# Early attention products over 128 rows and an output stored by groups: predicting one change to a fused attention and MoE kernel

## The chip, the core and the metric

The kernel runs on one core of one Trainium2 chip. The metric is the device time of one execution, in microseconds (us). The engines are named as in the profile: PE is TensorE (matmuls; PEld is its weight load), DVE is VectorE, ACT is ScalarE, POOL is GpSimd, SP is SyncE, whose queue issues nearly all DMAs here. DMAs that one engine issues start in the order in which they stand in its queue, and an issue that must wait holds back those behind it.

## The reference, cut to what matters

```python
def _attn_ref(q, k, v, s):                     # 4 x 8 heads, 576 positions, head size 64
    scores = (1.0 / np.sqrt(D)) * np.matmul(q, k.transpose(0, 1, 3, 2))
    cum = np.cumsum(np.maximum(s, 0.0), axis=-1)
    bias = -(cum[:, :, :, None] - cum[:, :, None, :])
    scores = np.where(causal, -1000000000.0, scores + np.minimum(bias, 0.0))
    attn = softmax(scores)
    return np.matmul(attn, v)

def reference(**kwargs):
    x = attn_out.transpose(0, 2, 1, 3).reshape(2304, 512)
    x = _moe_ref(x)     # RMS norm, then (silu(x @ w_gate) * (x @ w_val)) @ w_out
    return _moe2_ref(x) # the same without the norm, with other weights
```

All inputs are float32; the widths are 512 (model) and 1536 (hidden).

## The kernel before, in words

The work has four parts, one after the other with overlap: attention, the first MoE's gate and value products, its output product, and the second MoE. Activations are held transposed: 128 features on the partitions, up to 512 positions along the free dimension. Most products are made from values split in two parts (names ending in H and L), in the type fp32r; the early attention products are plain float32, which the trace shows as two PE instructions per product.

**The early quads.** The first 128 positions of each head need only a 128x128 block of scores. `EarlyQuad` does four heads at a time, eight quads in all (4 batches, and heads 0 to 3 or 4 to 7). Per head, L907 multiplies q (64 rows, the head size) by k, and L910 adds the cumulated `s` by a product of a unit column with the tile `heights` (64 rows too: 32 heads, as H and L parts). Quad 0 of a batch has its data in partitions 0 to 63, quad 1 in 64 to 127, so that one load of 512 KB (L895, tile `eq`) serves both, and each product uses half of the rows of the array. Then DVE takes the minimum with the mask (L915), ACT the exponential (L920), PE transposes (L932), ACT or DVE copies out (L936, L937), PE multiplies by the values (L941, 128 rows, tile `ev`), and the result is copied to `x` (L951, L952). After four quads `normalise` (squares L975, sums L982, factors L1035 to L1085, the normalised parts L1089 to L1094) makes the operands of the first MoE for half of the 512 early positions. The products of the first MoE on these early positions (group E, L1105, 256 columns each for the first five of 12 weight blocks) follow, with tanh on ACT (L1112) and two products on DVE (L1114, L1117). Ahead of the quads PE runs ten products on a cleared tile (L543).

**Weights.** `load_gv` brings the first MoE's weights through `convert`: a load (L464, tile `raw`), a copy on ACT (L468), a merge on DVE (L470), the H part on ACT or POOL (L475, L476), the L part on DVE or POOL (L479). `raw_places` puts the raw block f into the buffers of weight block f + 2; the tiles `eq` and `ev` sit in buffers of later blocks (`early_q`, `early_v`), so a raw load waits until the early tile in its place has been used.

**The order of the work.** Every operation is entered with a priority and an estimated length. `Plan.run` steps through time with these lengths and fixes, for each engine, the order in which its instructions stand. On the chip each engine follows that order and waits where data are late.

**The end.** The second MoE's output is made by `strassen_out`, twice, in blocks of 512 columns, and `plain_out`. The columns stand in groups: group E holds the early positions of all batches, the others hold runs of positions (`SPANS`: group, first column, length, output group, place in it, token). `store_out` writes each block of 128 x 512 with one DMA per run (L1834), to the tokens' places in the transposed output, so that the host only transposes.

```python
w=[(f"out{gi}", (d0, at))], pri=-1.0e4)      # L1834: the run at..at+n of group gi
```

Of the kernel before, what the change touches and what calls it, by code (L numbers as in the profile page):

```python
# [23 lines left out]
P = 128  # L24
# [27 lines left out]
def f32(ap):  # L52
    return ap.bitcast(F32)
# [267 lines left out]
FIRST = 1  # L321
# [4 lines left out]
def tile_kernel(  # L326
# [175 lines left out]
    early_q = [buf("w", f"{z}{f}", [P, 4, 2, P], F32, "eq") for f in (10, 11) for z in "HL"]  # L502
    early_v = [buf("w", f"{z}{f}", [P, NH, 2, D], F32, "ev") for f in (8, 9) for z in "HL"]
# [9 lines left out]
    def setup():  # L513
# [4 lines left out]
        for i, v in enumerate(early_v):  # L518
            def pad(en, v=v):
                for z in range(2):  # L520
                    en.memset(v()[:, z::2, 1 - z], 0.0)
            op([(POOL, 520), (DVE, 620)], 0, pad, w=[(v, "pad")], pri=-1.2e6 + i)
        def units_(en):
            for r in (0, 64):
                en.tensor_tensor(
                    out=unit()[r:r + 64], in0=ident()[r:r + 64, r:r + NB * NH],
                    in1=ident()[r:r + 64, r + NB * NH:r + 2 * NB * NH], op=ALU.add)
        op(POOL, 300, units_, r=[ident], w=[unit], pri=-1.35e6)
# [13 lines left out]
        for _ in range(10):  # L542
# [14 lines left out]
        def cumulate(en):  # L557
# [6 lines left out]
            for r in (0, 64):  # L564
                en.tensor_copy(cumHL()[r:r + NB * NH], c32())
            for r in (NB * NH, 64 + NB * NH):
                en.tensor_tensor(out=cumHL()[r:r + NB * NH], in0=c32(),
                                 in1=f32(cumHL()[:NB * NH]), op=ALU.subtract)
        op(DVE, 1700, cumulate, r=[cum], w=[cum, cum2, c32, cumHL], pri=-1e6)
# [308 lines left out]
    class EarlyQuad:  # L878
# [5 lines left out]
        def __init__(self, i, x):  # L884
# [5 lines left out]
            self.ql, self.vl, self.p = early_q[self.b], early_v[self.b], early_p[i % 2]  # L890

        def load(self, pri):
            b, ql, vl = self.b, self.ql, self.vl
            if self.j == 0:
                op(SP, 4 * P * 1024, lambda en: en.dma_start(  # L895
                    out=ql(), in_=qe[b].rearrange("j d h z p -> (j d) h z p")), w=[ql], pri=pri)
# [4 lines left out]
        def scores(self, pri):  # L901
            pt = ps_ring("sps", 2)
            rows = slice(D * self.j, D * self.j + D)
            for h in range(4):
                c = slice(P * h, P * h + P)
                n = 4 * self.i + h
                op(PE, (0.422 * 4 * P, D), lambda en, h=h, c=c: en.matmul(  # L907
                    pt()[:, c], self.ql()[rows, h, 0], self.ql()[rows, h, 1],
                    start=True, stop=False), r=[self.ql], w=[pt], pri=pri)
                op(PE, (C_TR, D), lambda en, c=c, n=n: en.matmul(  # L910
# [1007 lines left out]
```

## Time and profile before

| | |
|---|---|
| median of 3 runs | 1071.48 us (1068.91 to 1071.85) |
| the profiled execution | 1073.27 us, of it 1071.5 us from the first to the last instruction |
| PE busy | 1051.1 us (98%) |
| DVE, ACT, POOL busy | 762.9, 631.1, 265.5 us |
| mean granted TensorE clock | 0.989 of 2.4 GHz |
| DMA | 211.01 MB, 197 GB/s over the span |

The page gives busy times for the whole span. A busy PE need not be PE at its best: a matmul's time doubles when the granted clock is 1.2 GHz instead of 2.4 GHz, and both count as busy. So the places to read are the granted clock by stretch, the length of one product in the chain of waits, and the waits of PE by stretch.

### The profile page before, as it was taken

How to read it: one execution, taken by the hardware profiler on the slowest of the kernel's cores; microseconds unless marked ns; L12 is line 12 of the kernel's file. 1: busy time of each engine (PE TensorE's matmuls, PEld its weight loads, DVE VectorE, ACT ScalarE, POOL GpSimd, SP SyncE). 2: the span in 40 equal slices, each digit the busy share in tenths (PEclk: the TensorE clock that was granted, in tenths of full speed). 3: DMA queues.
4: the chain of work that ended last, by engine and by line, in shares of the span. 5: the costliest groups of instructions: out<-in, count | busy, mean ns of one | idle time of the engine just before them, and what ended most of it. 6: DMA issues, size and time to landing. Idle time of an engine off the chain costs nothing.

```text
span 1071.5 us, 17574 instructions
## 1 busy us (share of the span) xinstructions
PE 1051.1 (98%) x5512; PEld 912.1 (85%) x5512; DVE 762.9 (71%) x1749; ACT 631.1 (59%) x1315; POOL 265.5 (25%) x351
## 2 busy tenths in 40 slices
PE   9989999999999999999999999999999999999998
PEld 8878888998999899899877889888888888887777
DVE  4578988777777887558878887656777667964552
ACT  3678887676677465334456766555665455664542
POOL 1166876345355230100000000221222122200000
PEclk9699999999999999999999999999999999999999
DMA  9464554334244685368887662676667767877663
GB/s 317 140 214 143 169 154 124 117 113 138 90 150 127 199 272 168 102 211 293 271 297 222 207 203 95 209 224 215 226 216 239 257 218 250 304 245 220 203 202 112
DMA packets 130204, 211.01 MB, mean 197 GB/s; under 512 B 22400, under 2 KB 56960, under 8 KB 130112
## 3 DMA queue, kind: packets, MB, share of 16 engines
q1 hardware_dynamic: 129488, 209.57, 60.4%
q8 instruction: 43, 0.70, 0.3%
q14 instruction: 49, 0.40, 0.1%
q10 hardware_dynamic: 624, 0.34, 0.1%
HBM read 145.29 MB, written 64.56 MB: 196 GB/s over the span
## 4 chain that ended last, share of the span: by engine, by line
PE 78%; DVE 7%; DMA 6%; issue 3%; ACT 3%; SPq 2%; POOL 1%; ACTq 0%; DVEq 0%; POOLq 0%
PE mo L1105 24%; PE mo L1467 9%; PE mo L1638 7%; PE sps L1638 6%; PE tp L778 4%; PE tp L1467 4%; PE sps L696 3%; PE tp L766 3%; PE sps L1467 2%; PE mo L1714 2%; DMA raw<-in_w_gv 2%; PE sps L1105 1%; PE tp L1105 1%; PE sps L907 1%; PE mo L941 1%
## 5 line engine op out<-in xcount | busy, mean ns | idle before, releaser
L1387 DVE TENSOR_TENSOR hL<-hh,hH 128x512 fp32r<-128x512 f32 (+1 forms) x192 | 125.1, 667 | 77.4 <-ACT hH L1384 75.8
L1105 PE MATMUL mo<-xL,H 128*128 128x448 f32 (+2 forms) x472 | 169.8, 361 | 2.8 <-ACT t L1112 1.6
L1105 PE MATMUL mo<-xH,H 128*128 128x448 f32 (+2 forms) x472 | 171.1, 363 | 0.9 <-ACT t L1112 0.5
L1384 ACT ACTIVATE hH<-hh 128x512 fp32r<-128x512 f32 (+1 forms) x192 | 114.5, 602 | 97.5 <-DVE hL L1387 15.5
L1105 PE MATMUL mo<-xH,L 128*128 128x448 f32 (+2 forms) x472 | 170.2, 361 | 1.6 <-ACT t L1112 1.0
L1467 PE MATMUL mo<-hH,wo 128*128 128x512 f32 x312 | 97.6, 389 | 0.0
L1105 PEld LDWEIGHTS mo<-xL,H 128*128 128x128 f32 x472 | 88.7, 188 | 9.4 <-ACT t L1112 1.8
L1105 PEld LDWEIGHTS mo<-xH,H 128*128 128x128 f32 x472 | 88.8, 188 | 8.6 <-ACT t L1112 0.9
L1105 PEld LDWEIGHTS mo<-xH,L 128*128 128x128 f32 x472 | 88.7, 188 | 8.5 <-issue 1.4
L733 ACT ACTIVATE sc<-sc,col 128x256 f32<-128x256 f32 (+2 forms) x96 | 60.5, 631 | 38.0 <-DVE col L722 37.6
L1467 PEld LDWEIGHTS mo<-hH,wo 128*128 128x128 f32 x312 | 58.6, 188 | 12.1
L771 DVE TENSOR_TENSOR pTB<-tp,pTB 128x512 fp32r<-128x512 f32 (+1 forms) x96 | 56.5, 596 | 12.2 <-ACT pTB L769 11.8
L1467 PE MATMUL tp<-hH,wo 128*128 128x512 f32 x192 | 60.9, 391 | 2.6 <-ACT hH L1384 2.6
L1467 PE MATMUL mo<-hL,wo 128*128 128x512 f32 x156 | 60.8, 390 | 0.0
L769 ACT ACTIVATE pTB<-tp 128x512 fp32r<-128x512 f32 (+1 forms) x96 | 49.0, 520 | 19.0 <-PE tp L766 18.5
L1644 ACT ACTIVATE u<-sps 128x512 f32<-128x512 f32 x48 | 28.5, 594 | 53.3 <-PE sps L1638 53.3
L1467 PE MATMUL sps<-hH,wo 128*128 128x512 f32 x168 | 54.7, 399 | 3.5 <-ACT hH L1384 3.5
L778 PEld LDWEIGHTS tp<-pTB,vst 128*128 128x128 f32 x320 | 52.6, 189 | 3.3
L778 PE MATMUL tp<-pTB,vst 128*128 128x448 f32 (+3 forms) x320 | 54.4, 314 | 0.0
L766 PE MATMUL tp<-ident,sc 128*128 128x128 f32 x320 | 51.4, 273 | 0.8 <-DVE x L786 0.8
L1112 ACT ACTIVATE t<-mo 128x448 f32<-128x448 f32 (+2 forms) x59 | 30.6, 519 | 35.0 <-PE mo L1105 34.7
L1114 DVE SCALAR_TENSOR_TENSOR t<-t,mo 128x448 f32<-128x448 f32 (+2 forms) x59 | 34.8, 590 | 21.7 <-ACT t L1112 14.2
(287 smaller groups left out, 2804.7 us busy)
## 6 DMA issues: line engine op xcount, KB each, us to landing
raw<-in_w_gv SPq DMA_DIRECT2D x44, 511.8 KB, 5.6
tb<-h_d SPq DMA_DIRECT2D x48, 256.0 KB, 3.8
t<-tb SPq DMA_DIRECT2D x48, 256.0 KB, 3.1
hh<-t SPq DMA_DIRECT2D x48, 256.0 KB, 3.3
lq<-in_qk SPq DMA_DIRECT2D x32, 288.0 KB, 3.1
cb<-cum_d SPq DMA_DIRECT2D x32, 288.0 KB, 3.5
hh<-h_d SPq DMA_DIRECT2D x36, 256.0 KB, 3.1
row0B<-u SPq DMA_DIRECT2D x24, 256.0 KB, 3.2
```

What stands on the lines that cost most here:

```text
L696: op(PE, c_mm(n), lambda en, pt=pt, at=at, c=c, n=n, z=z, kk=kk: en.matmul(pt()[:, :n], qst[j]()[:, at:at + 128], kk()[:, c:c + n], start= ...
L733: op(ACT, c_act(o + m, 2) + 35, lambda en: en.activation(sc()[:m, :o + m], sc()[:m, :o + m], ACTF.Exp, scale=-1.0, bias=col()[:m, 0, t:t + 1],
L766: op(PE, C_TR, lambda en, pt=pt, a=a, kb=kb, t=t: en.transpose(pt()[:, a * P:a * P + P], self.sc[t]()[:, kb * P:kb * P + P], ident()), r=[ ...
L769: op(ACT, c_act(n), lambda en, pt=pt, c=c: en.activation(place(H, c), source(pt, c), ACTF.Copy), r=[pt], w=[(H, c)], pri=pri)
L771: op(DVE, c_tt(n), lambda en, pt=pt, c=c: en.tensor_tensor(out=place(L, c), in0=source(pt, c), in1=f32(place(H, c)), op=ALU.subtract), r=[ ...
L778: op(PE, c_mm(n), lambda en, w=w, z=z, kb=kb, d0=d0, n=n, o=o: en.matmul(po()[:, o:o + n], vst[j]()[:, kb, :], pT[z]()[:, d0:d0 + n], star ...
L1105: op(PE, c_mm(n), lambda en, a=a, x=x, c=c, k=k, i=i: en.matmul(ps()[:, :n], a()[:, c], x(k, lo, n), start=(k == 0 and i == 0), stop=(k == ...
L1114: op(DVE, c_tt(n), lambda en: en.scalar_tensor_tensor(out=t()[:, :n], in0=t()[:, :n], scalar=1.0, in1=gp()[:, :n], op0=ALU.add, op1=ALU.mu ...
L1384: op(ACT, c_act(n) + 35, lambda en: en.activation(H(), src(), ACTF.Copy), r=[src, *after], w=[H], pri=pri)
L1387: lambda en: en.tensor_tensor(out=L(), in0=src(), in1=f32(H()), op=ALU.subtract),
L1467: op(PE, c_mm(n), lambda en, m=m, w=w, xx=xx, kk=kk, i=i: en.matmul(ps[m]()[:, :n], w(), xx(), start=first and kk == 0 and i == 0, stop=kk ...
L1638: op(PE, c_mm(n), lambda en, w=w, xx=xx, cut=cut, kk=kk, i=i: en.matmul(ps()[:, :n], W[w]()[:, cut], xx(), start=first and kk == 0 and i == 0,
```

## The change

The early quads get operands of 128 rows. The host lays out `qe` per quad as six blocks: four blocks with q of one head, in rows 0 to 63 or 64 to 127 by turns and zeros in the other rows, and two blocks in which k of two heads is stacked. L907 and L910 so use all 128 rows; the unit columns and `heights` are cleared in their lower half (POOL) instead of being filled twice, which takes away a copy and a subtraction on DVE. The load becomes one of 384 KB per quad (eight) instead of one of 512 KB per batch (four). `early_q` takes the eight buffers of blocks 8 to 11, `early_v` those of blocks 6 and 7. There are 11 products ahead of the quads instead of ten, and the first weight block gets an earlier place in the plan (10 for 13.5). At the end, the output is stored by groups, 128 x 512 at a time in one DMA, and the host puts the columns in order. All lengths that the planner is told for the early products are now full.

```diff
@@ -318,7 +318,6 @@
 
 TINY = 70
 
-FIRST = 1
 HALVES = 5
 
 
@@ -499,8 +498,8 @@
 
 
 
-    early_q = [buf("w", f"{z}{f}", [P, 4, 2, P], F32, "eq") for f in (10, 11) for z in "HL"]
-    early_v = [buf("w", f"{z}{f}", [P, NH, 2, D], F32, "ev") for f in (8, 9) for z in "HL"]
+    early_q = [buf("w", f"{z}{f}", [P, 6, P], F32, "eq") for f in range(8, KF) for z in "HL"]
+    early_v = [buf("w", f"{z}{f}", [P, NH, 2, D], F32, "ev") for f in (6, 7) for z in "HL"]
     early = [buf("at", f"pTB{i}", [P, 1536], F32, f"early{i}") for i in range(2)]
     early_p = [Part(b, "p", lambda t: t[:, 1024:1536]) for b in early]
     cum = Part(early[0], "cum", lambda t: t[:NB * NH, :S])
@@ -520,12 +519,14 @@
                 for z in range(2):
                     en.memset(v()[:, z::2, 1 - z], 0.0)
             op([(POOL, 520), (DVE, 620)], 0, pad, w=[(v, "pad")], pri=-1.2e6 + i)
+
         def units_(en):
-            for r in (0, 64):
-                en.tensor_tensor(
-                    out=unit()[r:r + 64], in0=ident()[r:r + 64, r:r + NB * NH],
-                    in1=ident()[r:r + 64, r + NB * NH:r + 2 * NB * NH], op=ALU.add)
-        op(POOL, 300, units_, r=[ident], w=[unit], pri=-1.35e6)
+            en.memset(f32(unit()[64:]), 0.0)
+            en.memset(f32(cumHL()[64:]), 0.0)
+            en.tensor_tensor(
+                out=unit()[:64], in0=ident()[:64, :NB * NH],
+                in1=ident()[:64, NB * NH:2 * NB * NH], op=ALU.add)
+        op(POOL, 500, units_, r=[ident], w=[unit, (heights, "clear")], pri=-1.35e6)
         for x in (xs, xL[0], *xH):
             op(NONE, 0, lambda en, x=x: x.bufs[0](), w=[])
         op(ACT, 450, lambda en: en.dma_start(out=cum(), in_=s), w=[cum], pri=-3e6, later=2000)
@@ -539,7 +540,7 @@
         op(DVE, 150, lambda en: en.memset(zero()[:, 384:], 0.0), w=[zero], pri=-4e6)
         op(DVE, 200, clear, w=[*totE, *totals], pri=-0.9e6)
         first = mo_bank()
-        for _ in range(10):
+        for _ in range(11):
             op(PE, 216, lambda en: en.matmul(
                 first()[:, :P], zero()[:, 384:], zero()[:, 384:], start=True, stop=True),
                r=[zero], w=[first], pri=-1e6)
@@ -561,12 +562,10 @@
                                   op1=ALU.max)
             en.tensor_scalar(out=c32(), in0=cum2(), scalar1=cum2()[:, P // 2:P // 2 + 1],
                              scalar2=1.0 / SCALE, op0=ALU.subtract, op1=ALU.mult)
-            for r in (0, 64):
-                en.tensor_copy(cumHL()[r:r + NB * NH], c32())
-            for r in (NB * NH, 64 + NB * NH):
-                en.tensor_tensor(out=cumHL()[r:r + NB * NH], in0=c32(),
-                                 in1=f32(cumHL()[:NB * NH]), op=ALU.subtract)
-        op(DVE, 1700, cumulate, r=[cum], w=[cum, cum2, c32, cumHL], pri=-1e6)
+            en.tensor_copy(cumHL()[:NB * NH], c32())
+            en.tensor_tensor(out=cumHL()[NB * NH:2 * NB * NH], in0=c32(),
+                             in1=f32(cumHL()[:NB * NH]), op=ALU.subtract)
+        op(DVE, 1300, cumulate, r=[cum], w=[cum, cum2, c32, cumHL], pri=-1e6)
 
         def later():
             def selectors(en):
@@ -887,29 +886,28 @@
             self.col = cols[nunit[0] % 4]
             nunit[0] += 1
             self.sc = ring("at", "sc3", 2, [P, 512], F32)
-            self.ql, self.vl, self.p = early_q[self.b], early_v[self.b], early_p[i % 2]
+            self.ql, self.vl, self.p = early_q[i], early_v[self.b], early_p[i % 2]
 
         def load(self, pri):
             b, ql, vl = self.b, self.ql, self.vl
+            op(SP, 4 * P * 768, lambda en: en.dma_start(out=ql(), in_=qe[b, self.j]),
+               w=[ql], pri=pri)
             if self.j == 0:
-                op(SP, 4 * P * 1024, lambda en: en.dma_start(
-                    out=ql(), in_=qe[b].rearrange("j d h z p -> (j d) h z p")), w=[ql], pri=pri)
                 for z in range(2):
                     op(SP, 6 * P * 256, lambda en, z=z: en.dma_start(
                         out=vl()[:, z::2, z], in_=ve[b, :, z]), w=[(vl, z)], pri=pri + 1 + 0.1 * z)
 
         def scores(self, pri):
             pt = ps_ring("sps", 2)
-            rows = slice(D * self.j, D * self.j + D)
             for h in range(4):
                 c = slice(P * h, P * h + P)
                 n = 4 * self.i + h
-                op(PE, (0.422 * 4 * P, D), lambda en, h=h, c=c: en.matmul(
-                    pt()[:, c], self.ql()[rows, h, 0], self.ql()[rows, h, 1],
+                op(PE, 0.422 * 4 * P, lambda en, h=h, c=c: en.matmul(
+                    pt()[:, c], self.ql()[:, h], self.ql()[:, 4 + h // 2],
                     start=True, stop=False), r=[self.ql], w=[pt], pri=pri)
-                op(PE, (C_TR, D), lambda en, c=c, n=n: en.matmul(
-                    pt()[:, c], unit()[rows, n:n + 1].to_broadcast([D, P]), cumHL()[rows],
-                    start=False, stop=True), r=[unit, cumHL], w=[pt], pri=pri)
+                op(PE, C_TR, lambda en, c=c, n=n: en.matmul(
+                    pt()[:, c], unit()[:, n:n + 1].to_broadcast([P, P]), cumHL(),
+                    start=False, stop=True), r=[unit, cumHL, (heights, "clear")], w=[pt], pri=pri)
             for h in range(4):
                 c = slice(P * h, P * h + P)
                 op(DVE, c_tt(P), lambda en, h=h, c=c: en.tensor_tensor_reduce(
@@ -1238,7 +1236,7 @@
         attend_early(i)
     last_setup()
     for f in range(KF):
-        at = (13.5, 14.1, 14.2, 14.3, 14.4)[f] if f < HALVES else 18.1 + 0.9 * (f - HALVES)
+        at = (10, 14.1, 14.2, 14.3, 14.4)[f] if f < HALVES else 18.1 + 0.9 * (f - HALVES)
         early = at if f < HALVES else 17.4 + 0.7 * (f - HALVES)
         W1.append(load_gv(w_gv, f, places, tmps1, P_ATT + at, P_ATT - 1000 + early))
     moe1("E", (xH[0], xL[0]), W1, P_MOE, -1.0e4)
@@ -1829,11 +1827,10 @@
         def store(src, half, g):
             for m in range(2):
                 d0 = (2 * half + m) * P
-                for _, _, n, gi, at, t0 in SPANS:
-                    if gi == 2 * p + g:
-                        op(SP, 4 * P * n, lambda en, m=m, d0=d0, t0=t0, n=n, at=at: en.dma_start(
-                            out=outT[d0:d0 + P, t0:t0 + n], in_=src[m]()[:, at:at + n]),
-                           r=[src[m]], w=[(f"out{gi}", (d0, at))], pri=-1.0e4)
+                gi = 2 * p + g
+                op(SP, 4 * P * 512, lambda en, m=m, d0=d0, gi=gi: en.dma_start(
+                    out=outT[d0:d0 + P, 512 * gi:512 * gi + 512], in_=src[m]()),
+                   r=[src[m]], w=[(f"out{gi}", d0)], pri=-1.0e4)
         return store
 
     def rows2(p):
@@ -1846,7 +1843,6 @@
     strassen_out(rows2(1), WO, ring, two_banks("tp0", "tp1"), two_mo(), two_banks("sps0", "sps1"),
                  [t[4], t[5], t[2], t[3]], P4 + 100, 1.0, store_out(1))
     xr = wide(X_TAGS[1][3], [P, KD, 256], F32, "oo")
-    last0 = next(t0 for *_, gi, _, t0 in SPANS if gi == 4)
 
     def store_rest(xo, ps, dd):
         for z, e in enumerate((DVE, ACT)):
@@ -1857,7 +1853,7 @@
                 ACT: lambda en, c=c: en.activation(xo()[:, c], ps()[:, c], ACTF.Copy)}[e],
                r=[ps], w=[part], pri=-1.0e4)
             op((SP, ACT)[z], 4 * P * 128 if z == 0 else 450, lambda en, c=c: en.dma_start(
-                out=outT[dd * P:(dd + 1) * P, last0:last0 + 256][:, c], in_=xo()[:, c]),
+                out=outT[dd * P:(dd + 1) * P, 2048:2304][:, c], in_=xo()[:, c]),
                r=[part], w=[("out4", (dd, z))], pri=-1.0e4)
     plain_out(lambda f: (rest_d[f], [("rest_d", f)]), WO, ring, [mo_bank() for _ in range(4)],
               [Part(xr, k, lambda t, k=k: t[:, k, :]) for k in range(KD)], P4 + 200, 1.0, store_rest)
@@ -1890,11 +1886,15 @@
         cut = 448 - 64 * z
         qk[:, z::2, :, 0, :cut - P] = q[:, z::2, :, P:cut]
         qk[:, z::2, :, 0, cut + 64 - P:QW] = q[:, z::2, :, cut:]
+    qe = np.zeros((NB, 2, 2, D, 6, P), q.dtype)
+    for z in range(2):
+        qe[:, :, z, :, z:4:2] = q[:, z::2, :, :P].reshape(NB, 2, 2, D, P).transpose(0, 1, 3, 2, 4)
+        qe[:, :, z, :, 4:] = (qk[:, z::2, :, 1, :P].reshape(NB, 2, 2, D, P)
+                              .transpose(0, 1, 3, 2, 4))
+    qe = qe.reshape(NB, 2, P, 6, P)
     arrays = {
         "qk": np.ascontiguousarray(np.concatenate([qk, qk], axis=2)),
-        "qe": np.ascontiguousarray(
-            np.stack([q[..., :P], inputs["k"].transpose(0, 1, 3, 2)[..., :P]], axis=3)
-            .reshape(NB, 2, 4, D, 2, P).transpose(0, 1, 3, 2, 4, 5)),
+        "qe": qe,
         "ve": np.ascontiguousarray(
             v[:, :, :P].reshape(NB, NH // 2, 2, P, D).transpose(0, 3, 2, 1, 4)),
         "vp": np.ascontiguousarray(vp.reshape(NB, NH, 5, P, D).transpose(0, 1, 3, 2, 4)),
@@ -1914,4 +1914,7 @@
     with tile.TileContext(nc) as tc:
         tile_kernel(tc, *args)
     r = run_bass_kernel_spmd(nc, [{f"in_{n}": a for n, a in arrays.items()}], core_ids=[0])
-    return np.ascontiguousarray(r.results[0]["out_0_dram"].T)
+    out = np.empty((NT, DM), np.float32)
+    for _, _, n, gi, at, t0 in SPANS:
+        out[t0:t0 + n] = r.results[0]["out_0_dram"][:, 512 * gi + at:512 * gi + at + n].T
+    return out
```

How the change moves instructions, at three places. The line numbers of the changed kernel differ by one to three: L533 is L532 of before, L893 and L897 are L895 and L898, L463 is L464, L905 and L908 are L907 and L910, L930 is L932, L1440 is L1442, L1831 is L1834. The numbers in the names tell one tile from the next.

SP's queue at the start, from the load of `gcol` (L532) on; first before:

```order
L532 DMA gcol<-in_rms_g 128x4
L895 DMA eq<-in_qe 128x1024
L898 DMA ev<-in_ve 128x4x64 x2
L464 DMA raw_292<-in_w_gv 128x2047
L464 DMA raw_306<-in_w_gv 128x2047
L464 DMA raw_326<-in_w_gv 128x2047
L464 DMA raw_353<-in_w_gv 128x2047
```

and now:

```order
L533 DMA gcol<-in_rms_g 128x4
L893 DMA eq<-in_qe 128x768
L463 DMA raw_286<-in_w_gv 128x2047
L463 DMA raw_302<-in_w_gv 128x2047
L893 DMA eq<-in_qe 128x768
L897 DMA ev<-in_ve 128x4x64 x2
L893 DMA eq<-in_qe 128x768
L463 DMA raw_372<-in_w_gv 128x2047
L463 DMA raw_390<-in_w_gv 128x2047
```

Two loads of `eq` and one pair of `ev` now stand behind the first two weight loads (`raw`), which come ahead of the last quads' data.

PE's queue in the quads, about the end of the third quad; first before:

```order
L907 MATMUL sps_195<-eq 128x128
L910 MATMUL sps_195<-heights 128x128
L907 MATMUL sps_195<-eq 128x128
L910 MATMUL sps_195<-heights 128x128
L932 MATMUL tp_212<-ident,sc_197 128x128
L907 MATMUL sps_216<-eq 128x128
L910 MATMUL sps_216<-heights 128x128
L907 MATMUL sps_216<-eq 128x128
L910 MATMUL sps_216<-heights 128x128
L907 MATMUL sps_216<-eq 128x128
L932 MATMUL tp_212<-ident,sc_197 128x128 x3
```

and now:

```order
L930 MATMUL tp_217<-ident,sc_197 128x128 x2
L905 MATMUL sps_224<-eq 128x128
L908 MATMUL sps_224<-heights 128x128
L905 MATMUL sps_224<-eq 128x128
L908 MATMUL sps_224<-heights 128x128
L905 MATMUL sps_224<-eq 128x128
L908 MATMUL sps_224<-heights 128x128
L930 MATMUL tp_217<-ident,sc_197 128x128 x2
L905 MATMUL sps_224<-eq 128x128
L908 MATMUL sps_224<-heights 128x128
L930 MATMUL tp_245<-ident,sc_221 128x128 x3
```

The products, the transposes and their kinds are the same; the transposes of a quad stand earlier among the scores of later quads.

SP's queue in the last output block of 512 columns but one (tiles `row1B` and `row1T` are its operands); first before:

```order
L1442 DMA hh<-row1B_101 128x512 x4
L1834 DMA out_dram<-oo 128x128 x2
L1834 DMA out_dram<-oo 128x64
L1834 DMA out_dram<-oo 128x128
L1834 DMA out_dram<-oo 128x64
L1834 DMA out_dram<-oo 128x128 x2
L1834 DMA out_dram<-oo 128x64
L1834 DMA out_dram<-oo 128x128
L1834 DMA out_dram<-oo 128x64
L1442 DMA hh<-row1B_101 128x512
L1442 DMA hh<-row1T_106 128x512 x6
```

and now:

```order
L1440 DMA hh<-row1B_101 128x512
L1831 DMA out_dram<-oo 128x512 x2
L1440 DMA hh<-row1B_101 128x512 x5
L1440 DMA hh<-row1T_106 128x512
L1831 DMA out_dram<-oo 128x512 x2
L1440 DMA hh<-row1T_106 128x512 x5
```

The eight or ten stores that stood between the loads of operands are two in their place.

## Rows read from the trace of the kernel before

**Rows 1.** The page: busy time and share by engine; granted clock in 40 slices.

```profile
PE 1051.1 (98%) x5512; PEld 912.1 (85%) x5512; DVE 762.9 (71%) x1749; ACT 631.1 (59%) x1315; POOL 265.5 (25%) x351
...
PEclk9699999999999999999999999999999999999999
```

**Rows 2.** Windows: us; PE, PEld, DVE, ACT, POOL busy (count); PEclk, DMA share, GB/s.

```profile
6.90:17.70 10.80, 10.80 (x51) 9.29 (x51) 5.36 (x30) 4.94 (x24) 0.00 (x0) 1.00 1.10 349
17.70:20.40 2.70, 2.70 (x14) 2.53 (x12) 0.42 (x1) 0.00 (x0) 0.00 (x0) 1.00 1.03 414
20.40:27.20 6.80, 6.80 (x49) 5.55 (x47) 4.31 (x23) 3.80 (x15) 0.00 (x0) 1.00 0.80 315
27.80:47.40 19.60, 19.60 (x83) 17.25 (x84) 8.86 (x41) 10.41 (x37) 2.93 (x4) 0.50 0.35 103
47.70:51.40 3.70, 3.58 (x27) 2.95 (x24) 3.36 (x13) 3.33 (x9) 0.50 (x1) 0.97 0.78 223
```

**Rows 3.** Chain of waits, 6 to 60 us: start, us, what ended last.

```profile
6.20 0.23 DVE heights L565
...
6.45 0.29 DVE heights L567
...
7.33 0.53 PE sps L907 x2
...
17.82 2.00 PE mo L941 x8
...
21.10 1.09 PE mo L941 x8
22.18 0.25 PE sps L910
...
22.60 0.06 PE sps L910
22.66 0.27 PE sps L907 x2
...
44.09 3.43 PE mo L941 x16
...
59.96 2.54 PE mo L1105 x19
```

**Rows 4.** Windows: quads to the first tanh, and the E products behind it.

```profile
6.90:55.45 48.55, 48.39 (x250) 42.06 (x250) 27.01 (x117) 27.07 (x96) 5.45 (x7) 0.79 0.68 231
50.00:80.00 30.00, 25.20 (x181) 22.28 (x181) 23.20 (x48) 22.22 (x48) 18.93 (x19) 1.00 0.68 233
```

**Rows 5.** Timeline of ACT (start us, us, instruction): the first tanh of group E.

```profile
55.45 0.39 ACT L1112 ACTIVATE t<-mo 128x256 f32<-128x256 f32 x1
```

**Rows 6.** Timeline of SP's queue at the start.

```profile
9.18 7.93 SPq L464 DMA_DIRECT2D raw<-in_w_gv  x10
30.79 0.34 SPq L599 DMA_DIRECT2D cum_d<-early  x1
```

**Rows 7.** Windows: a halt of PE in the middle of the kernel.

```profile
560.00:562.00 2.00, 1.01 (x5) 0.51 (x3) 2.00 (x4) 0.38 (x1) 0.00 (x0) 1.00 1.01 384
...
564.00:566.00 2.00, 2.00 (x6) 1.60 (x5) 2.00 (x4) 0.96 (x2) 0.00 (x0) 0.50 0.63 185
```

**Rows 8.** Waits of PE, 960 to 1072 us: us in total, times, longest.

```profile
PE tp L1467 <- ACT hH L1384: 2.6, 2, 2.1
PE sps L1467 <- ACT hH L1384: 2.2, 2, 1.1
PE mo L1522 <- ACT hH L1384: 0.3, 1, 0.3
PE tp L1467 <- DVE hL L1387: 0.2, 1, 0.2
```

**Rows 9.** Timeline of SP's queue at the end.

```profile
1030.67 4.64 SPq L1834 DMA_DIRECT2D out_dram<-oo  x10
1035.41 0.38 SPq L1442 DMA_DIRECT2D hh<-row1B  x1
```

## The prediction, made before the changed kernel was timed

> **What bounds the kernel now.** The page says PE: busy 1051.1 us of 1071.5 [rows 1]. Only three things can then shorten the kernel: less work on PE, the same work at a higher clock, or less waiting of PE. So the next view is the granted clock by slice: it is at its upper level (2.4 GHz, shown as 9) nearly all the time, and low only in the second slice, near 27 to 54 us. The windows place it: 0.50, which is 1.2 GHz, from 27.8 to 47.4 us, though PE is busy in all 19.60 of 19.60 us [rows 2].
>
> The clock before 27 us has to be read from durations. The windows there show 1.00, but in the chain of waits one product of L907 takes 0.53 us at 7.33 us and 0.27 us at 22.66 us; eight instructions of L941 take 2.00 us at 17.82 and 1.09 us at 21.10 [rows 3]. That is the ratio of the two levels. So PE runs at 1.2 GHz from the first quad (6.9 us) to about 20.4 us, at 2.4 GHz to about 27.5 us, and again at 1.2 GHz to about 47.8 us: 13.5 and 20.3 us at the low level, all of it in the early quads.
>
> What did PE do before each change? In both low stretches it hardly stops, and most of its time goes to L907 and L910, over 64 rows. The clock rose behind the two stretches in which it had just run long series of L941, over 128 rows: 2.00 us of them at 17.82, 3.43 us at 44.09 [rows 3]. Since 10.80 busy us of 10.80 did not raise it [rows 2], busy time alone is not what does. I choose the reading that products over half of the rows count for little, which is what the change acts on. [...]
>
> The last view is the waits of PE at the end: 2.6 + 2.2 + 0.3 + 0.2 = 5.3 us from 960 us on, all for the split operands hH and hL [rows 8]. The queue of SP shows why: ten stores hold it from 1030.67 for 4.64 us, and only at 1035.41 is the next operand load issued [rows 9].
>
> **The change, part by part.** The sum is made against the profiled execution, 1073.27 us (span 1071.5). It lies 1.8 us above the median of the runs, 1071.48 us, from which I take the same sum off.
>
> 1. *The clock.* The trace has no 128-row L907, but its instructions have 128 columns as those of L941 do, and at 2.4 GHz two of L907 take 0.27 us, two of L941 1.09 / 4 = 0.27 us [rows 3]. So padding costs PE no time. If all the early products ran at 2.4 GHz, 13.5 + 20.3 = 33.8 us would become 16.9: **-16.9 us**.
>
> 2. *Until the clock is up.* It rose behind about 2 us of L941 and transposes once, behind 3.43 us another time. At best the 11 products ahead of the quads raise it (ten did not), which costs nothing; at worst 6 us of quads run at 1.2 GHz, which costs 3. I take 3 us of quads: **+1.5** (0 to 3).
>
> 3. *What is late next.* From 6.9 to 55.45 us, the first tanh [rows 5], PE has 48.39 us of work; less the 16.9 it is 31.5 us. ACT has 27.07 us in the same stretch and DVE 27.01 [rows 4], and the first tanh needs about the same conversions as before. So ACT and DVE, now half idle, would be busy 85% of the time behind PE, and each quad goes PE, DVE, ACT, PE, DVE or ACT, PE through two score buffers. The nearest row is 50 to 80 us: ACT 22.22, DVE 23.20 of 30 us, and PE idle for 4.8, or 16% [rows 4]. A sixth of 31.5 us is 5; the engines are denser still, so the bound is 6. The other bound is 0, as the scores of coming quads can fill gaps. I take the middle: **+3** (0 to 6).
>
> 4. *Switching between 64 and 128 rows.* L910 takes 0.25 us behind L941 and 0.06 in a series [rows 3]. There are 14 returns to the scores before, 12 after. If the 0.19 is due to the change of rows, up to 14 x 0.19 = 2.7 us go; if it is only the start of a series, nothing. I take **-1**. [...]
>
> 5. *Loads.* Eight loads of 384 KB for four of 512 KB are 1.05 MB more. At the 349 GB/s of the start [rows 2] that is 3.0 us, by which the third and later weight loads land later. SP issues ten weight loads from 9.18 to 17.1 us and then has nothing to do until 30.79 us [rows 6], which covers it; the ninth and tenth now also wait until the values of quads 1 and 3 are used, about 15 and 21 us at 2.4 GHz, inside that gap. **0**, and 3 if PE is there sooner than its weights.
>
> 6. *The start.* One copy of 0.23 us and one subtraction of 0.29 us fewer before the first L910 [rows 3]; one more product ahead of the quads, in time that PE waits for `heights`; two clears on POOL, hidden by the load of `s`. Under 0.3 either way, taken as 0.
>
> 7. *The stores.* 68 issues become 16. At 4.64 / 10 = 0.46 us each [rows 9] the eight or ten between operand loads become two, and the loads start 2.8 to 3.7 us sooner; the longest wait behind them is 2.1 us [rows 8]. Nearly all of the 5.3 us should go: **-4.5** (-2 if the loads then wait for the buffers instead, -5.3 at most).
>
> 8. *The rest.* The planner lays out everything anew from the new start. The work is the same, and what PE waits shifts: **+1** (-2 to +3), of the size of the 4.8 us that group E waits today [rows 4].
>
> The sum is -16.9 + 1.5 + 3 - 1 + 0 - 4.5 + 1 = -16.9 us: 1056.4 us for the profiled execution, **1054.5 us** for the median. The ends do not all fall together; taking the root of the sum of their squares, the case reaches from about 1049.5 to 1060.
>
> **The rivals.** *ACT and DVE become the bound.* The clock rises, but PE idles for the 6 us of step 3, the weights come the 3 us late of step 5, and the clock takes as assumed: -16.9 + 1.5 + 6 - 1 + 3 - 4.5 + 1 = -10.9, **1060.5 us**. For it: ACT and DVE at 74 and 77% already made PE idle [rows 4]. Against it: the conversions need not be done earlier than the products that use them.
>
> [...]
>
> *Slower: PE starves and the clock falls in group E.* PE would reach group E some 15 us sooner. If it then halts again and again for tanh and weights, the clock can fall there: in the middle of the kernel a halt of about 1 us in 560 to 562 is followed by 0.50 at 564 to 566 [rows 7]. The 240 products of 256 columns take 2.54 / 19 = 0.134 us each [rows 3], 32 us together, and 64 us at 1.2 GHz: 1054.5 + 32 = **1086.5 us**. It decides once about half of them run low (17 us lost). Against it: in 50 to 80 us PE idles 4.8 us in pieces, and the clock stays at 1.00 [rows 4].
>
> **How the numbers follow.** The forecast gets 0.77, the ACT and DVE case 0.12, the unanswering clock 0.08, the fall in group E 0.03. About four fifths of the first and half of the second lie within 1049.5 to 1060.5; 2 us more on each side bring the share to eight in ten: 1047.5 to 1062.5 us. About 0.3%, 3.2 us here, is what a measurement can tell from no change. The first two cases and most of the third are faster by more: 0.94. A store step worth little in the third case gives 0.03 for no change; the last case gives 0.03 for slower.
>
> **What would show it.** The granted clock should have no low stretch between 27 and 47 us, and one L905 should take 0.27 us from about 10 us on. The first tanh should come at 38 to 44 us instead of 55.45, with ACT busy for over 75% of the time before it. At the end PE's waits should fall to about 1 us and the stores appear as pairs of about 0.9 us. If L905 still takes 0.53 us at 15 us, the reading of the clock is wrong; if the first tanh is early and the end is not, what was won was given back in group E; if the waits at the end stay, it was not the stores' issue that they waited for.

## The result and the profile after

The changed kernel takes 1056.09 us (median of 4 runs, 1053.81 to 1058.95), against 1070.20 us for the kernel before beside it: a ratio of 0.9876 (95% interval 0.9835 to 0.9916). Ratios here are those of the recorded comparisons and can differ by up to 0.001 from the quotient of the medians. A second comparison gave 0.9849 (0.9821 to 0.9876). The forecast was 1054.5 us, range 1047.5 to 1062.5. The profiled execution is the slowest of the four, 1058.95 us with a span of 1056.8 us, 14.7 us less than before. All line numbers below are those of the changed kernel unless another is named.

The page, beside [rows 1]: PE has 14.6 us less busy time, and the granted clock has two dips, in the second slice (26 to 53 us) and in the 22nd (555 to 581 us).

```profile
PE 1036.5 (98%) x5514; PEld 905.4 (86%) x5514; DVE 766.9 (73%) x1746; ACT 631.3 (60%) x1312; POOL 263.8 (25%) x356
...
PEclk9799999999999999999998999999999999999999
```

The timeline of PE at the start and around the first dip (start us, us, engine, line, operands, count; in brackets the idle time ahead and what ended it). Where [rows 3] had 0.53 us for a pair of L907 alone, whole heads (a pair of L905 and the L908 behind it) of the first quad now start 0.34 us apart, from 6.36 us on. So the clock is at its upper level when the quads begin.

```profile
1.04 4.33 PE L544 MATMUL mo<-sq 128*128 128x128 f32 x22 [1.04 <-DVE sq L540]
...
6.36 0.30 PE L908 MATMUL sps<-heights 128*128 128x128 f32 x1 [0.76 <-DVE heights L566]
6.49 0.44 PE L905 MATMUL sps<-eq 128*128 128x128 f32 x2
6.68 0.31 PE L908 MATMUL sps<-heights 128*128 128x128 f32 x1
6.82 0.44 PE L905 MATMUL sps<-eq 128*128 128x128 f32 x2
...
28.07 0.39 PE L1073 MATMUL mo<-ident,sq 128*16 128x128 f32 x2 [0.55 <-DVE sq L1064]
...
31.03 0.77 PE L1083 MATMUL mo<-xH,sel 16*128 16x256 f32 x2 [0.76 <-DVE x L1087]
...
34.28 1.71 PE L980 MATMUL mo<-half,sq 128*128 128x2 f32 x8
...
37.27 0.41 PE L1103 MATMUL mo<-xL,H 128*128 128x256 f32 x1
37.48 0.41 PE L1103 MATMUL mo<-xH,L 128*128 128x256 f32 x1
```

The windows (us; PE, PEld, DVE, ACT, POOL busy with counts; PEclk, DMA share, GB/s) beside [rows 2, 4]: from the first head to the first tanh; the two halts; the stretch at a granted clock of 0.50; the second dip; the stretch near the end.

```profile
6.36:42.20 35.84, 34.48 (x250) 32.72 (x250) 26.80 (x113) 26.40 (x95) 7.42 (x12) 0.85 0.93 318
...
27.00:31.50 4.50, 3.18 (x22) 2.26 (x20) 3.52 (x14) 4.27 (x16) 1.07 (x5) 1.00 0.96 324
31.50:45.50 14.00, 13.53 (x60) 12.93 (x61) 7.71 (x18) 7.87 (x17) 3.83 (x4) 0.51 0.52 159
...
556.00:560.00 4.00, 4.00 (x11) 3.08 (x10) 3.66 (x6) 1.42 (x3) 0.00 (x0) 0.50 0.84 268
...
960.00:1040.00 80.00, 80.00 (x372) 67.04 (x371) 45.02 (x69) 43.30 (x74) 0.00 (x0) 1.00 0.74 228
```

The timeline of ACT has the first tanh (L1110) at 42.20 us, 13.25 us earlier than in [rows 5]. The same work lies ahead of it in both, down to 22 products of group E.

```profile
42.20 0.38 ACT L1110 ACTIVATE t<-mo 128x256 f32<-128x256 f32 x1 [3.38 <-PE mo L1103]
```

SP's queue near the end, beside [rows 9]: two stores where there were ten. The waits of PE for hH and hL [rows 8] are gone; the windows above show 80.00 of 80.00 us busy.

```profile
1020.02 1.02 SPq L1831 DMA_DIRECT2D out_dram<-oo  x2
1021.45 5.60 SPq L1440 DMA_DIRECT2D hh<-row1T  x5
```

Where the 14.7 us came from, by the same instructions in both timelines: the first tanh is 13.25 us earlier; the first output product (L1465) 8.9 us (525.0 to 516.1 us); the second MoE's last product ahead of the tail 5.6 us (915.2 to 909.6 us); the last instruction 14.7 us. So the early part won 13.25 us, gave back 7.65 on the way, and the tail won another 9.1. Three questions follow: is the tail's 9.1 us the stores' alone; what of the early gain went missing; and does the clock rest on rows?

### The profile page after: what moved, and what is told of

It reads as the page before. It is cut to its first block, busy times and chain, and to the rows that moved or that the text cites. A ratio compares the mean times of both kernels' runs of the same rounds, so it can differ in the third digit from the quotient of the medians.

```text
span 1056.8 us, 17525 instructions
## 1 busy us (share of the span) xinstructions
PE 1036.5 (98%) x5514; PEld 905.4 (86%) x5514; DVE 766.9 (73%) x1746; ACT 631.3 (60%) x1312; POOL 263.8 (25%) x356
## 4 chain that ended last, share of the span: by engine, by line
PE 82%; DVE 4%; DMA 3%; ACT 2%; issue 1%; ACTq 0%; SPq 0%; DVEq 0%
PE mo L1103 22%; PE mo L1465 10%; PE mo L1636 10%; PE sps L1636 9%; PE tp L1465 5%; PE tp L777 4%; PE sps L1465 4%; PE sps L695 3%; PE tp L765 3%; PE mo L1712 3%; PE mo L1520 2%; PE tp L1636 1%; DMA t<-tb 1%; PE sps L820 1%; PE sps L1103 1%
## 5 line engine op out<-in xcount | busy, mean ns | idle before, releaser
L1103 PE MATMUL mo<-xH,L 128*128 128x448 f32 (+2 forms) x472 | 172.6, 366 | 3.9 <-ACT t L1110 3.0
L1103 PE MATMUL mo<-xH,H 128*128 128x448 f32 (+2 forms) x472 | 172.0, 366 | 1.9 <-DVE t L1112 1.3
L1103 PE MATMUL mo<-xL,H 128*128 128x448 f32 (+2 forms) x472 | 171.6, 364 | 2.1 <-DVE t L1112 1.2
L1103 PEld LDWEIGHTS mo<-xH,L 128*128 128x128 f32 x472 | 90.4, 192 | 11.2 <-ACT t L1110 4.3
L1103 PEld LDWEIGHTS mo<-xL,H 128*128 128x128 f32 x472 | 90.4, 192 | 9.0 <-DVE t L1112 1.6
L1103 PEld LDWEIGHTS mo<-xH,H 128*128 128x128 f32 x472 | 90.2, 192 | 9.0 <-DVE t L1112 1.9
L1465 PE MATMUL mo<-hH,wo 128*128 128x512 f32 x312 | 97.8, 389 | 0.0
L1465 PEld LDWEIGHTS mo<-hH,wo 128*128 128x128 f32 x312 | 58.6, 188 | 12.2
L770 DVE TENSOR_TENSOR pTB<-tp,pTB 128x512 fp32r<-128x512 f32 (+1 forms) x96 | 56.4, 597 | 13.4 <-ACT pTB L768 12.6
L1465 PE MATMUL mo<-hL,wo 128*128 128x512 f32 x156 | 61.0, 391 | 0.0
L1465 PE MATMUL tp<-hH,wo 128*128 128x512 f32 x192 | 60.4, 389 | 0.0
L1110 ACT ACTIVATE t<-mo 128x448 f32<-128x448 f32 (+2 forms) x59 | 30.7, 520 | 46.2 <-PE mo L1103 40.7
L1465 PE MATMUL sps<-hH,wo 128*128 128x512 f32 x168 | 55.3, 403 | 2.2 <-ACT hH L1382 2.2
L1112 DVE SCALAR_TENSOR_TENSOR t<-t,mo 128x448 f32<-128x448 f32 (+2 forms) x59 | 34.9, 592 | 26.4 <-ACT t L1110 16.9
```

The costliest lines, as they stand in the source:

```text
L770: op(DVE, c_tt(n), lambda en, pt=pt, c=c: en.tensor_tensor(out=place(L, c), in0=source(pt, c), in1=f32(place(H, c)), op=ALU.subtract), r=[ ...
L1103: op(PE, c_mm(n), lambda en, a=a, x=x, c=c, k=k, i=i: en.matmul(ps()[:, :n], a()[:, c], x(k, lo, n), start=(k == 0 and i == 0), stop=(k == ...
L1112: op(DVE, c_tt(n), lambda en: en.scalar_tensor_tensor(out=t()[:, :n], in0=t()[:, :n], scalar=1.0, in1=gp()[:, :n], op0=ALU.add, op1=ALU.mu ...
L1465: op(PE, c_mm(n), lambda en, m=m, w=w, xx=xx, kk=kk, i=i: en.matmul(ps[m]()[:, :n], w(), xx(), start=first and kk == 0 and i == 0, stop=kk ...
```

## The experiments

Each kernel was timed beside the kernel before on the same chip; ratios are to that kernel, and since not all were timed on one chip, kernels are best compared by them.

| kernel | median us (runs) | ratio, 95% interval |
|---|---|---|
| stores alone | 1062.66 (6) | 0.9918, 0.9894 to 0.9942 |
| rows alone | 1065.02 (12) | 0.9934, 0.9912 to 0.9957 |
| unit products over 64 rows | 1071.33 (10) | 0.9995, 0.9967 to 1.0022 |
| one product ahead | 1066.10 (10) | 0.9949, 0.9928 to 0.9971 |
| both halts filled | 1052.85 (6) | 0.9819, 0.9787 to 0.9850 |
| both filled, wide sums | 1050.50 (6) | 0.9800, 0.9767 to 0.9833 |
| the change again | 1054.71 (4) | 0.9849, 0.9821 to 0.9876 |
| first halt filled | 1054.91 (5) | 0.9856, 0.9830 to 0.9882 |
| second halt filled | 1051.51 (4) | 0.9820, 0.9794 to 0.9845 |

**The stores alone.** The kernel before with this part of the diff (cut at the dots):

```diff
-                for _, _, n, gi, at, t0 in SPANS:
-                    if gi == 2 * p + g:
...
+                gi = 2 * p + g
+                op(SP, 4 * P * 512, lambda en, m=m, d0=d0, gi=gi: en.dma_start(
+                    out=outT[d0:d0 + P, 512 * gi:512 * gi + 512], in_=src[m]()),
...
```

and with the change's order of the columns on the host.

> The kernel before with the stores by groups of 512 and the host's reordering alone; the early part is untouched. Theory (read from the two traces): the stretch from 915.2 us to the end lost 9.1 us through the stores, so this kernel takes 1070.2 - 9.1 = about 1061 us (1059.5 to 1063), the first tanh stays at 55.4 us, and the 5.3 us of PE's waits behind 960 us are gone. Rival (step 7 of the prediction): only the 4.5 us of listed waits go, 1065.7 us (1064.5 to 1067), and the rest of what was won at the end came from the new layout of the early part.

Measured: 0.9918, which is 8.8 us of the 1072.33 us median beside it (the medians differ by 9.7); the first tanh at 55.12 us. The theory holds; the rival's 4.5 us lie outside the interval (6.2 to 11.4 us). The window near the end has no gap:

```profile
950.00:1040.00 90.00, 90.00 (x401) 74.56 (x400) 52.24 (x79) 48.54 (x82) 0.00 (x0) 1.00 0.76 231
```

Why 9 us, when the listed waits were 5.3? The timeline of the kernel before around its longest wait (same columns):

```profile
991.30 0.39 PE L1467 MATMUL tp<-hL,wo 128*128 128x512 f32 x1
991.53 0.39 PE L1467 MATMUL tp<-hH,wo 128*128 128x512 f32 x1
994.03 0.73 PE L1467 MATMUL tp<-hH,wo 128*128 128x512 f32 x2 [2.11 <-ACT hH L1384]
994.75 0.50 PE L1467 MATMUL tp<-hL,wo 128*128 128x512 f32 x1
995.09 0.63 PE L1467 MATMUL tp<-hH,wo 128*128 128x512 f32 x2
```

Products of 512 columns start 0.227 us apart when nothing is late, but each record is 0.39 us long, so the first 0.16 us of a wait is hidden under the record before it. Behind the wait the next starts are 0.72 (for two) and 0.34 us apart where 0.45 and 0.23 would do: 0.38 us more. So the listed 2.11 us cost 2.27 + 0.38 = 2.65. Summed in this way over 960 to 1045 us, starts were late by 9.0 us in all, three stalls without any listed wait among them; over 950 to 1030 us of the changed kernel, by none.

This kernel's trace also says something of the clock. Its early part is that of the kernel before, with ten products on the cleared tile, yet its clock is up when the quads begin. Its timeline of PE (line numbers of the kernel before) and a window:

```profile
6.90 0.29 PE L910 MATMUL sps<-heights 64*128 64x128 f32 x1 [1.18 <-DVE heights L567]
7.04 0.43 PE L907 MATMUL sps<-eq 64*128 64x128 f32 x2
7.23 0.30 PE L910 MATMUL sps<-heights 64*128 64x128 f32 x1
7.37 0.43 PE L907 MATMUL sps<-eq 64*128 64x128 f32 x2
...
8.51 0.73 PE L907 MATMUL sps<-eq 64*128 64x128 f32 x2
8.90 0.45 PE L910 MATMUL sps<-heights 64*128 64x128 f32 x1
9.15 0.73 PE L907 MATMUL sps<-eq 64*128 64x128 f32 x2
```

```profile
8.20:17.70 9.50, 9.50 (x43) 7.93 (x43) 4.25 (x27) 4.95 (x24) 0.00 (x0) 0.50 1.08 356
```

So the ten products raised the clock in this execution and not in that of [rows 3]. The quads over 64 rows then lost it: a head takes 0.33 us at 7.04 us and 0.64 at 8.51, and the level stays at 0.50 though PE is busy for 9.50 of 9.50 us. That they lost it is in line with step 1; the halt of 1.18 us just ahead of them may have a part in it. The 0.33 us of a head over 64 rows ahead of that fall, beside 0.34 over 128, also shows that the padding costs PE no time.

**The rows alone.** The changed kernel with the old store loop and the old return.

> The change without its stores: early products over 128 rows, output stored run by run as before. Theory: what the early part is worth once group E has given part of it back is read at 909.6 us, 5.6 us earlier than before: about 1064.5 us (1063 to 1066), first tanh at 42.2 us, waits of PE behind 960 us of about 5 us again. Rival (the prediction's steps without step 7): 12.4 us, about 1058 us (1056.5 to 1060).

Measured: 0.9934, 7.1 us of 1072.33; first tanh at 40.73 us, and the waits for hH back at 6.3 us. That is nearer to the theory's 5.6 than to the rival's 12.4. With the stores alone it makes 15.9 us, as the change together did (0.9876 and 0.9849: 13.3 and 16.2 us). Within the intervals the two parts add up, and the loss lies in the rows' part.

**The unit products over 64 rows.**

```diff
-                    pt()[:, c], unit()[:, n:n + 1].to_broadcast([P, P]), cumHL(),
+                    pt()[:, c], unit()[:64, n:n + 1].to_broadcast([64, P]), cumHL()[:64],
```

> The change with the unit products alone over 64 rows again, so that every head goes from 128 rows to 64 and back; the scores themselves stay padded. Theory A (step 4, a change of rows costs 0.19 us): a head of a quad, 0.34 us in the changed kernel, takes 0.53 to 0.72 us, 32 heads 6 to 12 us more, of which ACT and DVE hide some: 1060 to 1066 us. Theory B (the 0.25 us was only the start of a series): 0.34 us a head, 1056 us, within 1.5. Rival C (some products over 64 rows are enough to keep the clock down): a head takes 0.68 us at a granted clock of 0.50, first tanh 48 us or later, 1061 us or more.

Measured: 0.9995, the whole gain of the change lost with one operand's shape. As this kernel keeps the new stores, worth 8.8 us, its early part is some 8 us worse than that of the kernel before (an estimate from the two ratios). Its timeline of PE and its windows:

```profile
6.56 0.49 PE L905 MATMUL sps<-eq 128*128 128x128 f32 x2
6.98 0.32 PE L908 MATMUL sps<-heights 64*128 64x128 f32 x1
7.23 0.49 PE L905 MATMUL sps<-eq 128*128 128x128 f32 x2
...
12.76 0.80 PE L905 MATMUL sps<-eq 128*128 128x128 f32 x2
13.48 0.47 PE L908 MATMUL sps<-heights 64*128 64x128 f32 x1
13.88 0.80 PE L905 MATMUL sps<-eq 128*128 128x128 f32 x2
```

```profile
10.00:15.00 5.00, 5.00 (x17) 3.56 (x17) 0.93 (x8) 2.44 (x13) 0.00 (x0) 0.61 1.09 361
15.00:20.00 5.00, 5.00 (x18) 3.75 (x17) 1.62 (x9) 1.65 (x8) 0.00 (x0) 0.50 1.09 364
```

Theory A is right on the cost of a change and too low in the time; C is right on the clock and the time, and too low on the head. Before the clock falls a head takes 7.23 - 6.56 = 0.67 us where the change has 0.34: going from 128 rows to 64 and back costs 0.33 us here. And the clock falls at about 11 us, though PE is recorded as busy since the quads began (3.00 of 3.00 us from 7 to 10 us, 5.00 of 5.00 from 10 to 15); a head then takes 13.88 - 12.76 = 1.12 us, and the first tanh comes at 61.95 us. Whether the 64 rows or the changes between them let it fall is not told apart here.

**One product ahead of the quads.** In the changed kernel `range(11)` ahead of L544 becomes `range(1)`.

> The change with one cleared-tile product ahead of the quads where it has eleven. Theory: products over 128 rows raise the clock whatever their data, so with one ahead the quads do it themselves, later: L905 takes 0.53 us in the first quad and 0.27 us some 3 us later, 1.5 us more (0 to 3): about 1057.5 us. Rival 1: products of zeros did nothing, the clock rises at the same place as in the changed kernel, no difference. Rival 2: the quads cannot raise the clock by themselves, as before; L905 stays at 0.53 us to about 18 us, the first tanh is 5 to 7 us later, 1061 us or more.

Measured: 0.9949. The theory is right about the clock and wrong about the time. In its timeline the heads take 0.64 us to 9.78 us and 0.34 us after it:

```profile
9.14 0.74 PE L905 MATMUL sps<-eq 128*128 128x128 f32 x2
9.53 0.45 PE L908 MATMUL sps<-heights 128*128 128x128 f32 x1
9.78 0.59 PE L905 MATMUL sps<-eq 128*128 128x128 f32 x2
10.13 0.31 PE L908 MATMUL sps<-heights 128*128 128x128 f32 x1
10.27 0.44 PE L905 MATMUL sps<-eq 128*128 128x128 f32 x2
```

So here the quads over 128 rows raised the clock by themselves (0.64 to 0.34 us a head), which quads over 64 rows, with PE busy for 10.80 of 10.80 us, did not do from 6.9 to 17.7 us [rows 2]; and in the change eleven products of a cleared tile had done it before the quads began (0.34 us from the first head on), so products of zeros counted. The heads compared took 0.64 us each in both kernels and differ in their rows. The first tanh is still early, at 42.55 us. The time went later: the planner laid the work out in another order, the clock lies at 0.50 in the windows from 35 to 50 us, and one new wait of L695 takes 4.1 us; the clock is 0.93 from 60 to 110 us, where the change has 1.00. None of these was tried alone.

**Both halts filled.** This looks for the part of the early gain that went missing. The change with dummy products, in an order that is otherwise the same (`range` counts by quad and head; nobody reads the products):

```diff
+                def turn_(en, h=h, c=c):
+                    for _ in range({(7, 0): 2, (7, 3): 3}.get((self.i, h), 0)):
+                        en.matmul(pt()[:, c], ident(), ident(), start=True, stop=True)
+                    en.transpose(pt()[:, c], self.sc()[:, c], ident())
...
```

> The change, with five products of the identity with itself (two ahead of the last quad's first transpose, three ahead of its fourth), which nobody reads: they fill the two halts of PE at 27.5 us (0.55 us) and 30.3 us (0.76 us). Theory: the halts are what lets the clock fall at 31.9 us; with them filled it stays at 1.00 to 46 us, the 13.65 us of 0.50 in the changed kernel take half as long, and where ACT and DVE follow, the kernel takes 1049.5 to 1053.5 us. Rival 1: ACT and DVE set the pace there, the clock stays up but the waits of L1103 grow by as much: 1056 us, first tanh at about 42 us. Rival 2: the short products (L980's two columns, L1083's 16 rows) let it fall, halts or not: 0.50 from 32 to 45 us again, 1056 us.

Measured: 0.9819, 1052.85 us, within the theory's range; first tanh at 37.74 us, and the clock at 1.00 in each window up to 60 us. Rival 1 falls by the first tanh, which came earlier. Rival 2 falls: L980 (two columns) and L1083 (16 rows) are as short as before, and the clock stays at 1.00 from 30 to 45 us.

**Wide sums too.** `half`, the moving operand of L980, has 64 columns instead of two.

> The same with the sums of squares of group E over 64 columns, 62 of them of zeros, where L980 has two. Theory of the halts: as the kernel with the fills alone, within 1 us. Rival 2 (the two-column products count for little): the clock stays up here and not with the fills alone, and this kernel is 3 to 6 us faster than that one. Under either, if the 64 columns cost PE time of their own, the 32 passes take 0.12 us each before and at most 0.14 now: under 1 us.

Measured: 0.9800. The intervals of this kernel and the last overlap, the clock is at 1.00 up to 60 us in both, and eight passes take 1.00 us instead of 0.95. The first tanh is 1.1 us later (38.84 us), since PE waits for a load in the first quads:

```profile
8.77 0.49 PE L905 MATMUL sps<-eq 128*128 128x128 f32 x2 [1.16 <-DMA eq<-in_qe]
```

The width of the sums explains nothing here.

**One halt at a time, beside the change itself.** Of the five dummy products the first two or the last three are kept.

> The changed kernel itself, unaltered, beside the two that follow, since the first comparison had four runs of it: 0.9876 of the time before again, within its interval 0.9835 to 0.9916, and 4 to 6 us above the kernel with both halts filled (0.9819).

> Only the two products in the first halt (27.5 us, 0.55 us). Theory 1 (what counts is how much PE stands still before 31.9 us, together): the clock falls later or for a shorter time, and the gain is a part of that of both: 1 to 4 us. Theory 2 (the longer halt at 30.3 us decides): as the changed kernel, 0.50 from 32 to 45 us, the first tanh at 42 us. Theory 3 (the first halt decides): clock at 1.00 throughout, first tanh at 37.7 us, 0.982 of the time before.

> Only the three products in the second halt (30.3 us, 0.76 us). Theory 1: part of the gain, 1 to 4 us. Theory 2: clock at 1.00 throughout, first tanh at 37.7 us, 0.982 of the time before. Theory 3: 0.50 from 32 to 45 us, first tanh at 42 us, 0.9876.

Measured: the change 0.9849, the first halt filled 0.9856, the second 0.9820. The change lies only 3 us above the kernels with the second halt filled, not 4 to 6, but all four runs of the last (1048.93 to 1052.64 us) lie below all of the change (1053.32 to 1056.71 us). The five of the first halt filled reach from 1051.24 to 1057.45 us. Windows of the kernel with the first halt filled:

```profile
27.00:31.50 4.50, 3.62 (x27) 2.80 (x25) 3.51 (x17) 4.27 (x16) 1.07 (x5) 1.00 0.97 313
...
36.00:40.00 4.00, 4.00 (x21) 4.00 (x20) 1.84 (x5) 1.82 (x3) 0.00 (x0) 0.50 0.74 260
```

and of the one with the second filled, with its timeline of ACT (here L1114 and L1107 are the change's L1110 and L1103):

```profile
6.36:37.75 31.39, 30.54 (x256) 28.89 (x256) 25.93 (x113) 26.31 (x95) 6.58 (x11) 1.00 0.99 329
...
27.00:31.50 4.50, 3.86 (x28) 2.94 (x26) 3.53 (x14) 4.27 (x16) 1.06 (x5) 1.00 1.02 326
...
36.00:40.00 4.00, 3.53 (x29) 3.32 (x30) 3.02 (x9) 3.70 (x7) 2.09 (x2) 1.00 0.75 238
```

```profile
37.75 0.38 ACT L1114 ACTIVATE t<-mo 128x256 f32<-128x256 f32 x1 [0.19 <-PE mo L1107]
```

Theory 2 comes closest: with three dummy products at 30.0 us alone the clock stays at 1.00 and the first tanh comes at 37.75 us (41.68 in the change beside it); with two at 27.4 us it falls to 0.50. With those two the low stretch is shorter than in the change (0.78 from 31.5 to 36 us, 0.61 from 40 to 45.5 us), as theory 1 has it, but it is shorter yet with the rows alone, where nothing is filled, and the time is no better than the change's. The mean clocks of all executions agree with theory 2: in the 16 of the three kernels with the second halt filled it is 0.995 to 0.999; in the 13 without (the change in both comparisons, and the first halt filled) it is 0.990 to 0.994, but for two of 0.998, at 1053.81 and 1051.24 us. So, by these mean clocks, it fell with the second halt open in 11 of 13 executions, not in all. Whether it is the place or the larger fill (0.68 us against 0.44 of PE's busy time) is not told apart. This kernel, the change and three products, beats both kernels and is the simplest of those that do.

## Why the prediction was right, by its own steps

The time lay 1.6 us from the forecast. That it lay so near is in part luck: two terms were wrong by 4.6 and 6.65 us, in opposite directions. The mechanism of the largest term held.

- **Step 1, the clock (-16.9): the mechanism held.** The quads over 128 rows raised the clock (0.64 to 0.34 us a head with one product ahead); those over 64 did not raise it from 6.9 to 17.7 us [rows 2], and it fell under them where it was up (0.33 to 0.64 us a head with the stores alone), as it did under quads with mixed rows (0.67 to 1.12 us). The traces give the clock as a share, 1.00 and 0.50; no run shows the GHz that the step writes for the two levels, and its sum needs only their ratio (0.53 to 0.27 us for a pair of L907 [rows 3]). But 13.65 us of the early part still ran at a granted clock of 0.50, from 31.75 to 45.4 us, so the sign "no low stretch between 27 and 47 us" did not come true. With that fall prevented, the first tanh came 17.7 us earlier than before, about the size of step 1, though the 17.7 us also hold what steps 3, 4 and 6 gave and took.
- **Step 2, until the clock is up (+1.5):** it was nothing. Eleven products were enough before the quads began (0.34 us a head from the first on); with one, some 3 us of quads ran low (0.64 us a head up to 9.78 us), as the step assumed. Its "ten did not" was read from one execution; in the kernel with the stores alone ten did.
- **Step 3, what is late next (+3): right size, wrong cause for the quads.** ACT and DVE are not the bound before the first tanh: with the clock held they are busy for 26.31 and 25.93 of 31.39 us, 83 to 84%, near the 85% forecast, and PE for 30.54. In the change itself ACT is busy for 26.40 of 35.84 us, 74%, just under the 75% that the prediction had named as a sign. What came instead was the fall of the clock, 42.20 - 37.75 = 4.45 us. Steps 1 to 4 and 6 summed to -13.4; the trace has -13.25, with these errors cancelling.
- **Step 4, switching rows (-1):** too small a price. A change of rows and back costs 0.33 us (0.67 us a head with the unit products over 64 rows, 0.34 in the change), where the step priced each return at 0.19, and it is the change that costs, not the start of a series. At that price, taken at the upper level of the clock, the 14 returns cost up to 4.6 us before (an estimate); no run measures the term by itself.
- **Steps 5 and 6, loads and start (0):** no wait of PE for a load is listed up to 110 us in the change. The first L908 started 0.52 us earlier than the first L910 had (6.36 for 6.88 us), where step 6 allowed 0.3.
- **Step 7, the stores (-4.5): mis-sized, -9.1.** "Nearly all of the 5.3 us should go" took the listed waits for the whole cost. Late starts were 9.0 us.
- **Step 8, the rest (+1): mis-sized, +7.65.** Of this, 4.35 us lie between the first tanh and L1465: the 240 products of group E wait 7.9 us where they waited 5.3, nearly all for tanh and the products on DVE (below), and their records, counted once where they overlap, cover 39.1 us where they covered 35.1, by the low clock that lasts into them (2.2 of these 4.0 us lie ahead of the first tanh). With the second halt filled the records cover 35.5 us and the waits are still 7.9. So the ACT and DVE rival was right for group E, if not for the quads. Another 2.6 us lie between 516 and 564 us, where two waits of L1465 for hH and hL (2.21 and 0.92 us) and the dip of the clock behind them (0.50 from 556 to 560 us) make starts late by 6.9 us; before, by 4.4. ACT's step for the first waits 2.69 us for a load (`hh<-t`); these waits were not tried. The remaining 0.7 us is spread. Waits of PE in group E (us, times, longest), first before, then in the change:

```profile
PE mo L1105 <- ACT t L1112: 3.1, 4, 1.6
PE mo L1105 <- DVE t L1114: 2.2, 4, 0.6
...
PE mo L1103 <- ACT t L1110: 4.1, 9, 0.7
PE mo L1103 <- DVE t L1112: 3.3, 6, 0.9
```

- **The unanswering clock (0.08)** is out. PE busy for 10.80 of 10.80 us over 64 rows did not raise the clock [rows 2], while quads over 128 rows did (0.64 to 0.34 us a head); and with the unit products over 64 rows it fell to 0.50 though PE was busy for 5.00 of 5.00 us. And products of zeros counted: the first heads take 0.34 us behind eleven products of the cleared tile, 0.64 behind one.
- **The rival "PE starves and the clock falls in group E"** came true in part. The clock fell to 0.50, but behind two halts ahead of group E (0.55 and 0.76 us), and 13.65 us ran low, not the 64 us that the rival priced.

## What to carry to other kernels

Early products that used half of the array's rows left TensorE at its lower clock here (a pair of L907 at 0.53 us and 0.27 at the upper level [rows 3]), and padding the rows with zeros cost PE no time (0.34 us a head for 0.33); keep the rows of a series the same, as a change and back cost 0.33 us. Once such a stretch runs at full clock, look for the halts that are now exposed: three dummy products in one halt of 0.76 us were worth about 0.3%. And price a wait by how late the next instructions start, not by its listed idle time: here 2.11 us listed cost 2.65, and 5.3 us listed at the end cost 9.0.

## What the runs showed that was not expected

- Halts of 0.55 and 0.76 us within 4.5 us (PE busy 3.18 of 4.50 us) were followed by a low clock for 13.65 us; in the window around it PE was busy for 13.53 of 14.00 us, much of it with products over 128 rows. Why it stayed low under such steady work no run here explains. The same stretch was shorter in the kernel with the rows alone (0.64 from 36 to 40 us, 1.00 from 40 us on), whose early part is the same, so its length is not fixed.
- The windows show a clock of 1.00 at the start of the kernel with one product ahead, while a head takes 0.64 us there and 0.34 later: up to the first recorded change the level has to be read from durations.
